# Relu² attention and a feed-forward block on one core: attention steps merged into two per head pair, first weights averaged a chunk ahead, tokens kept in load order

## The chip, the core and the metric

One core of a Trainium2 chip runs the whole program. The metric is device microseconds (us) of one execution, the median of several. Engines are named as the profile names them: PE is TensorE's matmuls, PEld its weight loads, DVE is VectorE, ACT is ScalarE, POOL is GpSimd, SP is SyncE. The fast executions of one kernel in one set of rounds agree within 1.5 per cent here, most of them within one; an execution more than 1.5% above the fastest of its kernel is called slow and is left out of the ratios.

## The reference

```python
# q, k, v: (8, 12, 448, 64) float32; g_ln: (768,); w_ch1: (768, 3072); w_ch2: (3072, 768)
scores = (1 / sqrt(64)) * q @ k.T                    # per batch and head
attn   = relu(scores) ** 2 / 448
x      = (attn @ v).transpose(0, 2, 1, 3).reshape(8, 448, 768)
xn     = (x - mean(x)) / sqrt(var(x) + 1e-6) * g_ln  # over the last axis
out    = x + relu(xn @ w_ch1) @ w_ch2
```

## The kernel before

Heads are worked in pairs: 6 pairs in each of 8 batches, 48 in all. A pair goes through these steps on PE: `att_T` transposes its q and k (16 small matmuls), `att_QK(i, t)` makes scores for one of four groups of 112 keys (two matmuls; four such steps a pair), and `att_AV` multiplies by the values (8 matmuls) and accumulates. ScalarE applies the relu to each score tile, VectorE squares it, and VectorE writes the pair's result into `xT`, the transposed input of the feed-forward block.

The mean of the layer norm is folded into the first weights: `prep_w1` averages a chunk of `w1` (6 matmuls) and rewrites it with six VectorE operations. There are six chunks, and each is averaged once, during the first projection of batch 0. `ffn_1` is one block of the first layer (6 matmuls with a 448-wide operand), `ffn_x` transposes `xT` back to tokens for the residual, `ffn_2` is a quarter of an output tile of the second layer.

PE's order is fixed by the program. Attention steps are put between the blocks of the feed-forward layers.

```python
NJ = 4; SP = S // NJ                      # 4, 112: token = 4 * p + j
def load_batch(b, groups):                # q, k, v in `groups` equal pieces
    ...
def prep_w1(c):
    mean_ps = ps_f.tile([P, CH], fp32, tag="f")
    for ki in range(K1):
        nc.tensor.matmul(mean_ps, gmat[:, ki, :], w1[:, ki, c * CH:(c + 1) * CH], ...)
    for ki in range(K1):
        nc.vector.scalar_tensor_tensor(w1[:, ki, c * CH:(c + 1) * CH], ..., g_sb[:, ki:ki + 1], mean_ps,
                                       op0=Alu.mult, op1=Alu.subtract)
def att_QK(i, t):
    at = attn_pool.tile([SP, 2, S], bf16, tag="attn")     # 8 buffers
    sc = ps_sc.tile([P, 2, 512], fp32, tag="sc")          # 2 buffers
    ...                                                   # two matmuls
    nc.scalar.activation(at, sc[:SP, :, :S], Act.Relu)
    nc.vector.tensor_mul(at, at, at)
def att_AV(i):
    ps = ps_m.tile([P, S], fp32, tag="m")                 # 2 buffers, shared with att_T and ffn_x
    ...                                                   # eight matmuls
    nc.vector.tensor_scalar(
        xT[b][:, pr, :].rearrange("c (p j) -> c j p", j=NJ),
        ps[:, :].rearrange("c (j p) -> c j p", j=NJ), c2, None, op0=Alu.mult)
...
for i in range(NP_ALL):                                   # four excursions a pair
    att.append(att_T(i + 1));  att.append(att_QK(i, 0), att_QK(i, 1))
    att.append(att_AV(i - 1)); att.append(att_QK(i, 2), att_QK(i, 3))    # shortened
...
if u == 0 and bb == 0 and ni % (K2 // NCH) == 0:          # directly before the chunk's own blocks
    ffn.append((u * U + bb, 0.0, lambda c=ni // (K2 // NCH): prep_w1(c)))
...
load_batch(0, 3); load_batch(1, 2)                        # shortened
for c in range(2):
    load_w1(c)
```

## Time and profile before

| | before |
|---|---|
| median time | 640.27 us (3 runs, 639.38 to 642.77) |
| span of the profiled run, and its own time | 643.6 us, 645.38 us |
| mean granted clock of the profiled run | 0.981 |
| PE busy | 95% of the span |

From the page of the kernel before: the busy line, and four groups. A group's columns are line, engine, operation, output and inputs, shapes and count; then total busy us and mean ns; then the engine's idle time just before these instructions and what ended most of it.

```profile
PE 609.9 (95%) x4255; PEld 307.6 (48%) x4260; DVE 289.1 (45%) x476; ACT 283.6 (44%) x418; POOL 36.8 (6%) x49
...
L206 PE MATMUL ps<-xT_t,w_112 128*128 128x448 bf16 x1152 | 248.5, 362 | 14.8 <-DVE w_112 L117 13.9
...
L166 DVE TENSOR_SCALAR xT_t<-ps 128x448 bf16<-128x448 f32 x48 | 55.3, 1151 | 26.0 <-PE ps L161 25.9
...
L117 DVE SCALAR_TENSOR_TENSOR w_112<-w_112,g_sb,mean_ps 128x512 bf16<-128x512 bf16 x36 | 24.2, 739 | 1.3 <-PE mean_ps L114 1.3
```

The first layer (L206) waited 13.9 us for the scaling of its weights (L117). The write into `xT` (L166) takes 1.15 us each. An average over the span hides where this happens, so here is the table of windows of the kernel before: start and end, length, then busy us and instructions of PE, PEld, DVE, ACT and POOL, then granted clock, DMA share and GB/s.

```profile
0.00:36.00 36.00, 23.08 (x233) 12.25 (x234) 26.40 (x49) 23.06 (x27) 19.24 (x30) 1.00 1.23 170
36.00:60.00 24.00, 18.68 (x93) 7.03 (x94) 13.79 (x21) 7.36 (x12) 3.50 (x5) 0.93 1.33 203
60.00:90.00 30.00, 23.04 (x105) 8.49 (x107) 16.82 (x27) 10.00 (x15) 0.00 (x0) 0.83 0.87 157
90.00:121.00 31.00, 26.74 (x187) 12.00 (x187) 19.42 (x33) 17.05 (x24) 2.04 (x3) 0.83 0.34 45
...
160.00:640.00 480.00, 479.51 (x3348) 249.25 (x3346) 193.65 (x317) 199.95 (x299) 9.41 (x11) 1.00 0.20 40
```

From 160 us on PE is practically never idle (479.5 of 480 us). From 36 to 121 us it is busy 68.5 of 85 us, and part of that is at a lowered clock. So a gain in the first 121 us has to come from waits, and a gain after that has to come from PE's own work.

In the second part PE's own work still holds something to remove. The timeline of PE in the kernel before, in its steady part (start, duration, what ran):

```profile
140.82 2.44 PE L206 MATMUL ps<-xT_t,w_112 128*128 128x448 bf16 x12
143.19 0.59 PE L147 MATMUL sc<-qkT_t 64*112 64x448 bf16 x4
143.71 2.44 PE L206 MATMUL ps<-xT_t,w_112 128*128 128x448 bf16 x12
146.08 0.39 PE L133 MATMUL ps<-identity,q_sb 112*64 112x112 bf16 x8
```

From start to start, twelve first-layer matmuls take 2.37 us (143.19 less 140.82) and four score matmuls 0.52. Where 36 first-layer matmuls stand in a row they take 6.81 us, 0.189 each, so twelve alone should take 2.27. What is over comes with a change of tile shape (128x128 here, 64x112 and 112x64 in attention). Over the whole steady part in program order the prediction counts 483.7 us of matmul and 283 changes in 518.5 us; what is over gives 0.123 us a change.

Attention of batch 0 is bound by VectorE. Its timeline in one head pair of the kernel before:

```profile
20.44 1.17 DVE L150 TENSOR_TENSOR at<-at 112x896 bf16<-112x896 bf16 x2
21.54 0.61 DVE L139 COPY qkT_t<-ps 128x896 bf16<-128x896 bf16 x1
22.07 1.15 DVE L150 TENSOR_TENSOR at<-at 112x896 bf16<-112x896 bf16 x2
23.15 1.17 DVE L166 TENSOR_SCALAR xT_t<-ps 128x448 bf16<-128x448 f32 x1
```

There is no idle time in it, and the pattern repeats after 3.67 us (24.11, not shown, less 20.44).

### The profile page before, as it was taken

What the parts mean: (1) busy time and instruction counts of PE and PEld (TensorE: products, weight loads), DVE (VectorE), ACT (ScalarE), POOL (GpSimd) and SP (SyncE); (2) the same over time, 40 slices, a digit from 0 to 9 for tenths busy, and PEclk for the clock granted to TensorE, in tenths of its full rate; (3) what the DMA queues carried; (4) which work ended last, traced back from release to release, by engine and by line L of the source; (5) the groups of instructions that cost most, each with busy time, mean ns of one, the idle gap of its engine ahead of it and who ended that gap; (6) DMA issues with size and microseconds to landing.
All of it is one profiled execution on the core that took longest, in us unless ns stands there. A gap on an engine that the chain in (4) does not pass through costs nothing.

```text
span 643.6 us, 9809 instructions
## 1 busy us (share of the span) xinstructions
PE 609.9 (95%) x4255; PEld 307.6 (48%) x4260; DVE 289.1 (45%) x476; ACT 283.6 (44%) x418; POOL 36.8 (6%) x49
## 2 busy tenths in 40 slices
PE   4777878899999999999999999999999999999997
PEld 2422333444555544444555554444555555555664
DVE  4966455754545444455544443554554310112111
ACT  3933334766332346767433326676634105552000
POOL 7330001001000100001000100000000000000000
PEclk9989787999999999999999999999999999999999
DMA  9999910900641173006220813000001110000111
GB/s 130 201 203 206 210 26 0 129 1 4 109 74 44 50 111 43 0 2 87 32 62 25 135 36 58 2 1 1 1 25 50 49 50 2 0 1 25 50 50 49
DMA packets 45483, 37.59 MB, mean 58 GB/s; under 512 B 1920, under 2 KB 41856, under 8 KB 45440
## 3 DMA queue, kind: packets, MB, share of 16 engines
q0 software_dynamic: 40624, 25.96, 28.5%
q1 hardware_dynamic: 4816, 11.01, 4.4%
q8 instruction: 33, 0.54, 0.4%
q14 instruction: 10, 0.08, 0.0%
HBM read 51.91 MB, written 11.01 MB: 98 GB/s over the span
## 4 chain that ended last, share of the span: by engine, by line
PE 88%; DVE 9%; ACT 1%; DMA 1%; issue 1%; POOL 0%; POOLq 0%; ACTq 0%
PE ps L206 35%; PE o_ps L222 35%; PE sc L147 6%; PE ps L161 6%; DVE w_112 L117 4%; PE ps L133 3%; DVE at L150 2%; PE ps L190 2%; DVE xT_t L166 1%; DMA k_sb<-in_k_dram 1%; ACT at L149 1%; DVE qkT_t L139 1%; PE mean_ps L114 1%; DVE stats L197 0%; POOL q_sb L91 0%
## 5 line engine op out<-in xcount | busy, mean ns | idle before, releaser
L206 PE MATMUL ps<-xT_t,w_112 128*128 128x448 bf16 x1152 | 248.5, 362 | 14.8 <-DVE w_112 L117 13.9
L222 PE MATMUL o_ps<-w_113,h_114 128*128 128x384 bf16 x1344 | 230.9, 327 | 0.0
L149 ACT ACTIVATE at<-sc 112x896 bf16<-112x896 f32 x192 | 164.5, 918 | 129.6 <-PE sc L147 129.5
L150 DVE TENSOR_TENSOR at<-at 112x896 bf16<-112x896 bf16 x192 | 118.8, 624 | 156.5 <-ACT at L149 156.5
L208 ACT ACTIVATE h_114<-ps 128x448 bf16<-128x448 f32 x192 | 105.0, 547 | 167.4 <-PE ps L206 167.4
L206 PEld LDWEIGHTS <-w_112 128*128 128x128 bf16 x1152 | 107.3, 99 | 136.3 <-DVE w_112 L117 26.4
L222 PEld LDWEIGHTS <-h_114 128*128 128x128 bf16 x1344 | 125.7, 98 | 97.9 <-issue 19.0
L225 DVE SCALAR_TENSOR_TENSOR o_t<-o_ps,rstd_t,x_t 128x384 f32<-128x384 f32 x56 | 34.5, 616 | 74.2 <-PE o_ps L222 74.0
L166 DVE TENSOR_SCALAR xT_t<-ps 128x448 bf16<-128x448 f32 x48 | 55.3, 1151 | 26.0 <-PE ps L161 25.9
L147 PE MATMUL sc<-qkT_t 64*112 64x448 bf16 x384 | 59.8, 381 | 5.9 <-ACT at L149 5.9
L161 PE MATMUL ps<-at,v_sb 112*64 112x448 bf16 x384 | 48.5, 369 | 1.2 <-DVE at L150 0.5
L196 DVE BATCH_NORM_STATS2 stats<-x_t 128x6 f32<-128x384 bf16 x28 | 15.7, 561 | 64.0 <-ACT x_t L193 63.7
L139 DVE COPY qkT_t<-ps 128x896 bf16<-128x896 bf16 x48 | 29.8, 620 | 23.8 <-PE ps L133 23.3
L147 PEld LDWEIGHTS <-qkT_t 64*112 64x112 bf16 x384 | 19.7, 127 | 38.2 <-issue 36.9
L161 PEld LDWEIGHTS <-v_sb 112*64 112x64 bf16 x384 | 19.0, 112 | 26.6 <-issue 19.8
L133 PE MATMUL ps<-identity,q_sb 112*64 112x112 bf16 x384 | 19.4, 226 | 6.2 <-DMA q_sb<-in_q_dram 6.2
L117 DVE SCALAR_TENSOR_TENSOR w_112<-w_112,g_sb,mean_ps 128x512 bf16<-128x512 bf16 x36 | 24.2, 739 | 1.3 <-PE mean_ps L114 1.3
L193 ACT COPY x_t<-ps 128x768 bf16<-128x768 bf16 x28 | 22.5, 803 | 3.3 <-PE ps L190 3.3
L133 PEld LDWEIGHTS <-q_sb 112*64 112x64 bf16 x384 | 12.1, 113 | 21.1 <-issue 14.6
L91 POOL DMA_DIRECT2D q_sb<-in_q_dram x11 | 9.4, 859 | 217.8 <-PE ps L133 216.6
L133 PE MATMUL ps<-identity,k_sb 112*64 112x112 bf16 x384 | 18.3, 220 | 1.4 <-DMA k_sb<-in_k_dram 1.4
L91 POOL DMA_DIRECT2D v_sb<-in_v_dram x11 | 9.3, 844 | 117.1 <-PE ps L161 116.3
(23 smaller groups left out, 95.8 us busy)
## 6 DMA issues: line engine op xcount, KB each, us to landing
out_dram<-o_t SPq DMA_DIRECT2D x28, 384.0 KB, 2.3
w_112<-in_moe_w_ch_dram POOLq DMA_DIRECT2D x6, 768.0 KB, 22.0
w_113<-in_moe_w_ch_dram POOLq DMA_DIRECT2D x4, 1152.0 KB, 33.9
q_sb<-in_q_dram POOLq DMA_DIRECT2D x6, 672.0 KB, 7.3
k_sb<-in_k_dram POOLq DMA_DIRECT2D x6, 672.0 KB, 10.3
v_sb<-in_v_dram POOLq DMA_DIRECT2D x6, 672.0 KB, 7.2
q_sb<-in_q_dram POOLq DMA_DIRECT2D x3, 224.0 KB, 7.5
k_sb<-in_k_dram POOLq DMA_DIRECT2D x3, 224.0 KB, 8.0
```

What stands on the lines that cost most here:

```text
L117: nc.vector.scalar_tensor_tensor(w1[:, ki, c * CH:(c + 1) * CH], w1[:, ki, c * CH:(c + 1) * CH], g_sb[:, ki:ki + 1], mean_ps, op0=Alu.mult ...
L133: nc.tensor.transpose(ps[hh * D:(hh + 1) * D, t, j * SP:(j + 1) * SP], sb[:, 2 * pr + hh, j * D:(j + 1) * D], identity[:SP, :SP])
L139: nc.vector.tensor_copy(qkT[i], ps)
L147: nc.tensor.matmul(sc[:SP, hh, :S], qkT[i][r, 1, t * SP:(t + 1) * SP], qkT[i][r, 0, :], start=True, stop=True)
L149: nc.scalar.activation(at, sc[:SP, :, :S], Act.Relu)
L150: nc.vector.tensor_mul(at, at, at)
L161: nc.tensor.matmul(ps[hh * D:(hh + 1) * D, :], v_sb[:, 2 * pr + hh, t * D:(t + 1) * D], attn[i, t][:, hh, :], start=(t == 0), stop=(t == N ...
L166: nc.vector.tensor_scalar(xT[b][:, pr, :].rearrange("c (p j) -> c j p", j=NJ), ps[:, :].rearrange("c (j p) -> c j p", j=NJ), c2, None, op0 ...
L206: nc.tensor.matmul(ps, w1[:, ki, ni * P:(ni + 1) * P], xT[u * U + bb][:, ki, :], start=(ki == 0), stop=(ki == K1 - 1))
L208: nc.scalar.activation(h1[:, ni, bb * S:(bb + 1) * S], ps, Act.Relu)
L222: nc.tensor.matmul(o_sb[1], h1[:, ki, m * P:(m + 1) * P], w2[:, ki, j * hd:(j + 1) * hd], start=(ki == 0), stop=(ki == K2 - 1))
L225: nc.vector.scalar_tensor_tensor(o_sb[0][:, j * hd:(j + 1) * hd], o_sb[1], rstd[u][:, m:m + 1], x_tok[u][:, m, j * hd:(j + 1) * hd], op0=A ...
```

## The change

It has six parts. The four excursions per pair become two, and a pair's values stand next to the transposes of a later pair, because both have 112x64 tiles. The attention steps are spread by deadlines instead of by a rate. Each chunk's average stands a chunk ahead of its use, the first one inside batch 0's attention, with its own accumulator pool. `xT` keeps the order in which tokens are loaded, so the write is contiguous and the output goes out in two or three pieces. Half of batch 1's squares go to GpSimd. Loads of batch 0 come in groups of 2, 4 and 6 heads. The diff, cut to its core:

```diff
-    def load_batch(b, groups):               # equal groups
+    def load_batch(b, groups):               # for hs in groups: ...
...
     def prep_w1(c):
-        mean_ps = ps_f.tile([P, CH], fp32, tag="f")
+        mean_ps = ps_m.tile([P, CH], fp32, tag="m")
...
         nc.scalar.activation(at, sc[:SP, :, :S], Act.Relu)
-        nc.vector.tensor_mul(at, at, at)
+        eng = nc.gpsimd if (NPAIR <= i < 2 * NPAIR and t % 2 == 1) else nc.vector
+        eng.tensor_mul(at, at, at)
...
         nc.vector.tensor_scalar(
-            xT[b][:, pr, :].rearrange("c (p j) -> c j p", j=NJ),
-            ps[:, :].rearrange("c (j p) -> c j p", j=NJ), c2, None, op0=Alu.mult)
+            xT[b][:, pr, :], ps, c2, None, op0=Alu.mult)
...
-                nc.sync.dma_start(out_flat[r0:r0 + P, :], o_sb[0])
+                while c0 < (m + 1) * P:      # one piece per group of 112 columns
+                    ...
+                    nc.sync.dma_start(out_tok[u * U + bb, ..., jj, :], o_sb[0][...])
...
-        att.append((b, lambda i=i: (att_QK(i, 0), att_QK(i, 1))))
-        ...                                  # four excursions a pair
+    def step_a(i):
+        att_QK(i, 0)
+        att_QK(i, 1)
+    def step_b(i):
+        att_QK(i, 2)
+        att_QK(i, 3)
+        if i > 0:
+            att_AV(i - 1)
+        if i + 2 < NP_ALL:
+            att_T(i + 2)
...
-                if u == 0 and bb == 0 and ni % (K2 // NCH) == 0:
-                    ffn.append((u * U + bb, 0.0, lambda c=ni // (K2 // NCH): prep_w1(c)))
+                if u == 0 and bb == 0 and ni % CPN == 0 and ni // CPN + 1 < NCH:
+                    items.append((0.0, lambda c=ni // CPN + 1: prep_w1(c)))
...
-    load_batch(0, 3)
-    load_batch(1, 2)
-    for c in range(2):
+    load_batch(0, (2, 4, 6))
+    load_batch(1, (6, 6))
+    for c in range(NCH):
         load_w1(c)
...
+        while ai < steps_of(0):
+            if ai == steps_of(0) - 4:
+                prep_w1(0)
+            pull()
...                                          # then pull() whenever ai + 1 <= target(t)
```

More of the change, by code (lines that the diff above doesn't have):

```diff
@@ L45 @@
     c2 = (1.0 / D) / S
-    out_flat = out.rearrange("b s d -> (b s) d")
+    out_tok = out.rearrange("b (p j) d -> b p j d", j=NJ)
     const_pool = ctx.enter_context(tc.tile_pool(name="const", bufs=1))
@@ L87, in load_batch @@
         v_sb = io_pool.tile([SP, H, NJ * D], bf16, tag="v_sb")
-        hs = H // groups
-        for gi in range(groups):
+        h0 = 0
+        for hs in groups:
             for sb, src in ((q_sb, q), (k_sb, k), (v_sb, v)):
                 nc.gpsimd.dma_start(
-                    sb[:, gi * hs:(gi + 1) * hs, :],
-                    src[b, gi * hs:(gi + 1) * hs].rearrange("h (p j) d -> p h (j d)", j=NJ),
+                    sb[:, h0:h0 + hs, :],
+                    src[b, h0:h0 + hs].rearrange("h (p j) d -> p h (j d)", j=NJ),
                 )
+            h0 += hs
         qkv[b] = (q_sb, k_sb, v_sb)
@@ L228, in ffn_2 @@
             if j == 1:
-                r0 = u * UT + m * P
-                nc.sync.dma_start(out_flat[r0:r0 + P, :], o_sb[0])
-    att = []
-    NP_ALL = B * NPAIR
-    att.append((0, lambda: att_T(0)))
-    for i in range(NP_ALL):
-        b = i // NPAIR
-        if i + 1 < NP_ALL:
-            att.append((b, lambda i=i: att_T(i + 1)))
-        att.append((b, lambda i=i: (att_QK(i, 0), att_QK(i, 1))))
-        if i > 0:
-            att.append(((i - 1) // NPAIR, lambda i=i: att_AV(i - 1)))
-        att.append((b, lambda i=i: (att_QK(i, 2), att_QK(i, 3))))
@@ L244 @@
-    att.append((B - 1, lambda: att_AV(NP_ALL - 1)))
+                c0 = m * P
+                while c0 < (m + 1) * P:
+                    g0 = c0 // SP
+                    c1 = min((m + 1) * P, (g0 + 1) * SP)
+                    bb, jj = divmod(g0, NJ)
+                    nc.sync.dma_start(
+                        out_tok[u * U + bb, c0 - g0 * SP:c1 - g0 * SP, jj, :],
+                        o_sb[0][c0 - m * P:c1 - m * P, :])
+                    c0 = c1
+    NP_ALL = B * NPAIR
+    att = []
@@ L246, with steps_of @@
+    def step_a(i):
[8 more added lines that the diff above has]
+            att_T(i + 2)
+    for i in range(NP_ALL):
+        att.append(lambda i=i: step_a(i))
+        att.append(lambda i=i: step_b(i))
+    att.append(lambda: att_AV(NP_ALL - 1))
+    def steps_of(b):
+        return min(len(att), 2 * NPAIR * (b + 1) + 2) if b < B - 1 else len(att)
     NU = B // U
-    ffn = []
+    segs = []
@@ L248 @@
+    CPN = K2 // NCH
     for u in range(NU):
-        last = u * U + U - 1
         for bb in range(U):
+            items = []
             for ni in range(K2):
-                if u == 0 and bb == 0 and ni % (K2 // NCH) == 0:
-                    ffn.append((u * U + bb, 0.0, lambda c=ni // (K2 // NCH): prep_w1(c)))
-                ffn.append((u * U + bb, 1.12, lambda u=u, bb=bb, ni=ni: ffn_1(u, bb, ni)))
+                if u == 0 and bb == 0 and ni % CPN == 0 and ni // CPN + 1 < NCH:
+                    items.append((0.0, lambda c=ni // CPN + 1: prep_w1(c)))
+                items.append((1.12, lambda u=u, bb=bb, ni=ni: ffn_1(u, bb, ni)))
@@ L255 @@
                 if ni % 6 == 5:
-                    m = bb * 4 + ni // 6
-                    m -= 1 if bb == 0 else 1
+                    m = bb * 4 + ni // 6 - 1
                     if 0 <= m < MU:
-                        ffn.append((u * U + bb, 0.4, lambda u=u, m=m: ffn_x(u, m)))
+                        items.append((0.4, lambda u=u, m=m: ffn_x(u, m)))
+            segs.append((u * U + bb, items))
+        items = []
         for m in range(MU):
@@ L262 @@
                 for part in range(4):
-                    ffn.append((last, 0.96, lambda u=u, m=m, j=j, p=part: ffn_2(u, m, j, p, 4)))
-    load_batch(0, 3)
-    load_batch(1, 2)
+                    items.append((0.96, lambda u=u, m=m, j=j, p=part: ffn_2(u, m, j, p, 4)))
+        segs.append((u * U + U - 1, items))
+    load_batch(0, (2, 4, 6))
+    load_batch(1, (6, 6))
+    for c in range(NCH):
+        load_w1(c)
+    ai = 0
     nload = 2
-    for c in range(2):
-        load_w1(c)
     def pull():
-        nonlocal nload, ai
-        b, fn = att[ai]
-        fn()
+        nonlocal ai, nload
+        att[ai]()
@@ L275, in pull @@
         ai += 1
-        if ai < len(att):
-            done = att_done(ai)
-            while nload < B and nload - 2 < done:
-                load_batch(nload, 1)
-                nload += 1
-    last_av = {}
-    for n, (b, _) in enumerate(att):
-        last_av[b] = n
-    def att_done(n):
-        c = 0
-        while c < B and last_av[c] < n:
-            c += 1
-        return c
-    ai = 0
-    with tc.manual_schedule(engines={mybir.EngineType.PE}):
-        total = sum(c for need, c, _ in ffn if need < B - 2)
-        nfree = 0
-        credit = 0.0
-        wc = 2
-        w2c = 0
-        for n, (need, cost, fn) in enumerate(ffn):
-            while att_done(ai) <= need:
-                pull()
-            if nfree == 0:
-                nfree = len(att) - ai
-                rate = nfree / (total * 1.0)
-            fn()
-            if cost == 0.0:
-                if wc < NCH:
-                    load_w1(wc)
-                    wc += 1
-                elif w2c == 0:
-                    while w2c < W2C:
-                        load_w2(w2c)
-                        w2c += 1
-            credit += cost * rate
-            while credit >= 1.0 and ai < len(att):
-                pull()
-                credit -= 1.0
-        assert ai == len(att) and nload == B and w2c == W2C
@@ new lines, in pull, with target @@
+        while nload < B and ai >= steps_of(nload - 2):
+            load_batch(nload, (6, 6))
+            nload += 1
+            if nload == 3:
+                for c in range(W2C):
+                    load_w2(c)
+    with tc.manual_schedule(engines={mybir.EngineType.PE}):
+        att_T(0)
+        att_T(1)
+        while ai < steps_of(0):
+            if ai == steps_of(0) - 4:
+                prep_w1(0)
+            pull()
+        bounds = {}
+        total = 0.0
+        cum = []
+        for need, items in segs:
+            total += sum(c for c, _ in items)
+            cum.append(total)
+        t1 = cum[0]
+        t_end = cum[-1] - sum(c for c, _ in segs[-1][1]) - sum(c for c, _ in segs[-2][1])
+        n0, n1, n2 = steps_of(0), steps_of(1), len(att)
+        def target(t):
+            if t <= t1:
+                return n0 + (n1 - n0) * t / (t1 - 3.0)
+            return n1 + (n2 - n1) * (t - t1) / (t_end - 3.0 - t1)
+        t = 0.0
+        for need, items in segs:
+            while ai < steps_of(need):
+                pull()
+            for cost, fn in items:
+                fn()
+                t += cost
+                while ai < len(att) and ai + 1 <= target(t):
+                    pull()
+        assert ai == len(att) and nload == B
```

## The prediction

> **What bounds it now.** The page gives TensorE (PE) 95% of the 643.6 us span and 88% of the chain. By stage (table of windows, chain in order of time):
>
> - 0 to 36 us: attention of batch 0, bound by VectorE. Per head pair: four squares (0.5 us each), one strided write into xT (1.10), one transpose copy (0.54); 3.68 us a pair.
> - 36 to 121: first projection of batch 0. Each of six weight chunks is averaged on PE, scaled by six VectorE operations (4.05 us in a row) and used at once. PE waits for them (13.9 us in 30 waits); granted clock falls to 0.50 to 0.85 in several 5 us stretches. It ends with a VectorE-bound burst (110 to 121) that catches up batch 1's attention.
> - 121 to 640: PE without a gap. 36 first-layer matmuls take 6.81 us, 12 take 2.38: 0.19 each plus 0.12 whenever the next block has another tile shape. Four score matmuls take 0.52 for 0.38. The Trainium skill, "TensorEngine Tiling (Array Packing)", Key Properties, says a change of tiling mode drains the TensorE; the 0.12 agrees. In program order I count 483.7 us of matmul and 283 changes; at 0.123 each that gives the measured 518.5.
>
> **What changes.**
> 1. Four excursions per pair (8 changes) become two: scores; scores, values, transposes. Values and transposes share the column-tiled shape, so I count 5 changes. After batch 0's projection 283 become about 184: 99 x 0.123 = 12 us, all on the critical path.
> 2. The average moves a chunk ahead, so its 4 us of VectorE runs under PE work. A chunk then costs 24 matmuls (4.54), an average (1.29), a pair's attention (1.91) and changes: 8.4 us; six take 50, where 36 to 121 went by, and no catch-up burst remains.
> 3. The write into xT becomes contiguous: 1.10 to about 0.55 us, an estimate from the 0.62 of the 384-wide output operation. Batch 0's attention becomes ScalarE-bound: four relus of 0.865, 3.5 us a pair.
> 4. Half of batch 1's squares go to GpSimd. The skill, "GPSIMD Engine Reference", section 4.1, calls it about 2x slower for two-input elementwise; I estimate 2 to 2.5 us each. Needed a pair later, so hidden.
> 5. Outputs leave in two or three pieces per tile; tail unchanged.
>
> **The new cost.** The first average now stands in PE's order before pair 5. By the DMA rates in the windows (200 GB/s), q, k, v of two batches land at 26.5 us and weight chunk 0 near 30.5; PE is there at about 27.5 and waits 3 to 4 us. The six scalings then delay pair 5's squares, and the first projection starts near 41 instead of 36.5.
>
> **Sum.** First layer starts at 41, then 557 us of matmul and changes by the same count, 2 of small waits (the average needs an accumulator that xT's write frees), 4 of tail: span 604; the timed runs lie 3 below the span: 601 us, 6% faster. About 27 us come from the start, 12 from fewer changes.
>
> **Signs.** PE's waits on weight scaling vanish; a 2 to 5 us wait on the weight DMA appears near 28; clock 1.0 after 45 us; batch 0's projection ends near 92; blocks of score, value and transpose take 1.9 us; the xT write 0.5 to 0.65.
>
> **What would break it.** Score to value changes dearer than 0.123; GpSimd squares queued behind weight DMA issues, stalling the values of pairs 6 to 8; the clock staying low; ScalarE holding first-layer evictions.

## More of the kernel before

The span is what the profiler sees of one execution. The time of that same execution is 1.8 us longer.

## The result, and the profile after

| | before | after |
|---|---|---|
| median time of the same rounds | 641.52 us (4 runs, 639.38 to 643.46) | 622.73 us (4 runs, 620.59 to 623.85) |
| span of the profiled run | 643.6 us | 622.1 us |
| its own time | 645.38 us | 623.85 us |
| its granted clock | 0.981 | 0.988 |

The ratio is 0.9704, with a 95% interval of 0.9658 to 0.9749: faster by 3.0%. A ratio here and below is the mean time of one kernel's fast runs over that of the kernel before in the same rounds, so it is not quite the ratio of the medians that are quoted. The prediction said 601 us. The direction was right, the gain is half of what was forecast, and the time is 21.7 us above the predicted one.

The same lines of the page of the kernel after:

```profile
PE 588.5 (95%) x4254; PEld 316.8 (51%) x4260; DVE 259.6 (42%) x464; ACT 284.9 (46%) x418; POOL 68.3 (11%) x79
...
L208 PE MATMUL ps<-xT_t,w_112 128*128 128x448 bf16 x1152 | 231.1, 354 | 1.0 <-DVE xT_t L169 0.7
...
L169 DVE TENSOR_SCALAR xT_t<-ps 128x448 bf16<-128x448 f32 x48 | 29.4, 613 | 4.8 <-PE ps L164 4.8
...
L119 DVE SCALAR_TENSOR_TENSOR w_112<-w_112,g_sb,mean_ps 128x512 bf16<-128x512 bf16 x36 | 24.3, 741 | 6.4 <-PE mean_ps L116 6.4
```

The first layer lost its waits (14.8 to 1.0 us of idle time before it) and 17.4 us of busy time; fewer changes of shape and less time at a lowered clock would both act on it, and the page doesn't part them. The `xT` write fell from 1.15 to 0.61 us. These three signs are as predicted. The windows of the kernel after:

```profile
0.00:36.00 36.00, 20.62 (x187) 11.15 (x189) 19.46 (x39) 18.02 (x21) 18.93 (x30) 1.00 1.21 168
36.00:60.00 24.00, 16.67 (x128) 8.21 (x128) 19.95 (x26) 11.99 (x16) 13.01 (x11) 0.82 1.29 205
60.00:90.00 30.00, 27.42 (x189) 13.12 (x192) 21.09 (x35) 16.14 (x24) 12.03 (x10) 0.92 1.22 198
90.00:121.00 31.00, 30.44 (x234) 15.61 (x233) 19.07 (x32) 21.21 (x33) 6.06 (x5) 1.00 0.22 29
...
160.00:617.00 457.00, 455.31 (x3241) 248.07 (x3239) 163.58 (x304) 196.03 (x292) 15.20 (x20) 1.00 0.20 38
```

From 90 us on PE is nearly without a gap, as forecast. The first row is worse than before: in the first 36 us PE ran 187 matmuls where the kernel before ran 233. In the second it runs more than before (128 to 93), but it is idle for 7.3 us and its granted clock is 0.82. PE's waits in the kernel after (total us, times, longest), the groups that matter:

```profile
PE sc L149 <- ACT at L151: 7.0, 14, 0.8
...
PE mean_ps L116 <- DVE xT_t L169: 6.0, 4, 4.7
...
PE ps L192 <- DVE xT_t L169: 2.5, 3, 0.8
```

One of the waits of an average for an `xT` write is 4.7 us long. It ends at 60.52, and the next three fences show PE, DVE and POOL of the kernel after around it. A bracket gives the idle time before the instruction and what ended it.

```profile
60.52 0.59 PE L116 MATMUL mean_ps<-w_112,gmat 128*128 128x512 bf16 x1 [4.71 <-DVE xT_t L169]
61.33 1.91 PE L116 MATMUL mean_ps<-w_112,gmat 128*128 128x512 bf16 x4 [0.22 <-issue]
63.03 3.36 PE L208 MATMUL ps<-xT_t,w_112 128*128 128x448 bf16 x12
```

```profile
55.45 4.48 DVE L153 TENSOR_TENSOR at<-at 112x896 bf16<-112x896 bf16 x1 [1.97 <-ACT at L151]
59.86 0.61 DVE L169 TENSOR_SCALAR xT_t<-ps 128x448 bf16<-128x448 f32 x1
```

```profile
55.28 0.82 POOL L111 DMA_DIRECT2D w_113<-in_moe_w_ch_dram  x1 [0.94 <-DMA k_sb<-in_k_dram]
56.12 3.33 POOL L153 TENSOR_TENSOR at<-at 112x896 bf16<-112x896 bf16 x2
```

A square that elsewhere takes VectorE 0.62 us took 4.48 us. It ended at 59.93, 0.48 us after both GpSimd squares had ended (56.12 plus 3.33). Four other VectorE squares (at 44.67, 87.48, 95.50 and 97.93) met one on GpSimd; they took 1.25 to 1.90 us, and each ended 0.48 us after it. The `xT` write stood behind it on VectorE, the average of the third chunk stood behind that write, because it takes the accumulator that the write frees, and PE sat idle. After the gap twelve first-layer matmuls took 3.36 us instead of 2.43: the clock had dropped.

The slower start is seen on ScalarE, whose relus were to be the limit. Its timeline in the kernel after, one line for each head pair:

```profile
16.86 3.35 ACT L151 ACTIVATE at<-sc 112x896 bf16<-112x896 f32 x4 [0.53 <-PE sc L149]
22.24 3.35 ACT L151 ACTIVATE at<-sc 112x896 bf16<-112x896 f32 x4 [2.02 <-PE sc L149]
27.57 3.34 ACT L151 ACTIVATE at<-sc 112x896 bf16<-112x896 f32 x4 [1.98 <-PE sc L149]
31.38 3.34 ACT L151 ACTIVATE at<-sc 112x896 bf16<-112x896 f32 x4 [0.47 <-PE sc L149]
```

Four relus take 3.35 us, as predicted, but the pairs follow each other after 5.38, 5.33 and 3.81 us, because ScalarE waits for the next pair's scores. PE shows why, in the second of those pairs:

```profile
18.64 0.62 PE L149 MATMUL sc<-qkT_t 64*112 64x448 bf16 x2 [0.19 <-ACT at L151]
19.19 1.71 PE L164 MATMUL ps<-at,v_sb 112*64 112x448 bf16 x8
21.57 0.99 PE L149 MATMUL sc<-qkT_t 64*112 64x448 bf16 x4
```

Between the last scores of a pair and the first of the next stand the values and the transposes (19.19 to 21.57, the transposes of 0.59 us twice are not shown). Two score buffers keep ScalarE busy for two relus, 1.7 us, and PE took 2.4 us. Values took 1.71 us there and 0.95 at the full clock; four scores 0.99 and 0.59.

The steady part of the kernel after looks as intended: values and transposes follow each other without a change of shape.

```profile
166.22 0.58 PE L149 MATMUL sc<-qkT_t 64*112 64x448 bf16 x4
166.73 0.95 PE L164 MATMUL ps<-at,v_sb 112*64 112x448 bf16 x8
167.51 0.36 PE L135 MATMUL ps<-identity,q_sb 112*64 112x112 bf16 x8
```

Counted in program order, the whole program has 348 changes of shape before and 230 after.

### The profile page after: what moved, and what is told of

It reads as the page before. It is cut to its first block, busy times and chain, and to the rows that moved or that the text cites. A ratio compares the mean times of both kernels' runs of the same rounds, so it can differ in the third digit from the quotient of the medians.

```text
span 622.1 us, 9876 instructions
## 1 busy us (share of the span) xinstructions
PE 588.5 (95%) x4254; PEld 316.8 (51%) x4260; DVE 259.6 (42%) x464; ACT 284.9 (46%) x418; POOL 68.3 (11%) x79
## 4 chain that ended last, share of the span: by engine, by line
PE 88%; DVE 4%; ACT 3%; issue 2%; DMA 1%; POOL 1%; POOLq 0%; ACTq 0%
PE o_ps L224 36%; PE ps L208 35%; PE sc L149 7%; PE ps L164 5%; ACT at L151 3%; PE ps L135 3%; PE mean_ps L116 2%; DVE at L153 1%; PE ps L192 1%; DVE w_112 L119 1%; DMA k_sb<-in_k_dram 1%; DVE xT_t L169 1%; ACT x_t L195 0%; ACT h_114 L210 0%; POOL q_sb L92 0%
## 5 line engine op out<-in xcount | busy, mean ns | idle before, releaser
L208 PE MATMUL ps<-xT_t,w_112 128*128 128x448 bf16 x1152 | 231.1, 354 | 1.0 <-DVE xT_t L169 0.7
L224 PE MATMUL o_ps<-w_113,h_114 128*128 128x384 bf16 x1344 | 225.0, 326 | 0.0
L224 PEld LDWEIGHTS <-h_114 128*128 128x128 bf16 x1344 | 128.5, 98 | 89.4 <-issue 6.1
L208 PEld LDWEIGHTS <-w_112 128*128 128x128 bf16 x1152 | 108.7, 98 | 106.9 <-issue 11.8
L149 PE MATMUL sc<-qkT_t 64*112 64x448 bf16 x384 | 61.3, 390 | 7.0 <-ACT at L151 7.0
L164 PE MATMUL ps<-at,v_sb 112*64 112x448 bf16 x384 | 47.8, 372 | 0.4 <-DVE w_112 L119 0.4
L169 DVE TENSOR_SCALAR xT_t<-ps 128x448 bf16<-128x448 f32 x48 | 29.4, 613 | 4.8 <-PE ps L164 4.8
L92 POOL DMA_DIRECT2D q_sb<-in_q_dram x17 | 13.1, 769 | 149.7 <-PE ps L135 147.6
L92 POOL DMA_DIRECT2D v_sb<-in_v_dram x17 | 12.9, 761 | 134.4 <-PE ps L164 133.4
L135 PEld LDWEIGHTS <-q_sb 112*64 112x64 bf16 x384 | 16.5, 117 | 15.3 <-DMA q_sb<-in_q_dram 6.6
L153 POOL TENSOR_TENSOR at<-at 112x896 bf16<-112x896 bf16 x12 | 20.9, 1744 | 24.8 <-ACT at L151 24.8
```

The source lines that it names most:

```text
L135: nc.tensor.transpose(ps[hh * D:(hh + 1) * D, t, j * SP:(j + 1) * SP], sb[:, 2 * pr + hh, j * D:(j + 1) * D], identity[:SP, :SP])
L149: nc.tensor.matmul(sc[:SP, hh, :S], qkT[i][r, 1, t * SP:(t + 1) * SP], qkT[i][r, 0, :], start=True, stop=True)
L153: eng.tensor_mul(at, at, at)
L164: nc.tensor.matmul(ps[hh * D:(hh + 1) * D, :], v_sb[:, 2 * pr + hh, t * D:(t + 1) * D], attn[i, t][:, hh, :], start=(t == 0), stop=(t == N ...
L169: nc.vector.tensor_scalar(xT[b][:, pr, :], ps, c2, None, op0=Alu.mult)
L208: nc.tensor.matmul(ps, w1[:, ki, ni * P:(ni + 1) * P], xT[u * U + bb][:, ki, :], start=(ki == 0), stop=(ki == K1 - 1))
```

## The experiments

My theory after the trace: most of the missing 22 us lies before 63 us, and it comes in four pieces. The GpSimd squares hold VectorE; the merged order starves ScalarE in the start, made worse by a cold clock; the load groups 2, 4, 6 start the pairs late; and waits for `xT` writes come back wherever an average or a token transpose follows a merged block. Rivals: a change of shape is worth less than 0.123 us, so that merging gains little anywhere; the clock alone makes the start slow; the arrival of the first weight chunk alone paces it. All twelve kernels gave the reference's result. The runs came in three sets of four, each set on one chip with the kernel before; the medians of the kernel before were 641.42 (e1 to e4), 640.73 (e5 to e8) and 642.78 us (e9 to e12). Kernels of different sets, and after with any of them, are best compared by their ratios; differences of medians are given as such and can be off by a microsecond or two.

| run | edit | median us | ratio to before (95%) |
|---|---|---|---|
| e1_dve | after, no squares on GpSimd | 615.88 | 0.9609 (0.9571 to 0.9646) |
| e2_groups444 | after, loads of batch 0 in 4, 4, 4 | 622.32 | 0.9695 (0.9666 to 0.9724) |
| e3_split0 | after, pairs 1 to 6 in the old order | 616.15 | 0.9626 (0.9562 to 0.9690) |
| e4_four | after, four excursions everywhere | 625.16 | 0.9736 (0.9711 to 0.9762) |
| e5_defer | e1, average or token transposes not directly after a merged block | 614.78 | 0.9574 (0.9533 to 0.9614) |
| e6_warm | e1, filler matmuls in the start | 615.36 | 0.9587 (0.9542 to 0.9631) |
| e7_early | e1 + e2 + e3, first chunk loaded and averaged early | 616.22 | 0.9608 (0.9570 to 0.9645) |
| e8_best | e7 + e5 | 612.69 | 0.9557 (0.9518 to 0.9596) |
| e9_late | after, each chunk averaged directly before its use | 644.66 (one of four slow) | 1.0009 (0.9944 to 1.0074) |
| e10_strided | after, old `xT` write and output order | 624.93 | 0.9726 (0.9696 to 0.9756) |
| e11_split | e8, first chunk's scaling spread over the steps | 606.31 | 0.9435 (0.9406 to 0.9464) |
| e12_splitwarm | e11 + filler in the first 20 us | 608.59 | 0.9471 (0.9442 to 0.9500) |

### e1_dve: no squares on GpSimd

```diff
-        eng = nc.gpsimd if (NPAIR <= i < 2 * NPAIR and t % 2 == 1) else nc.vector
-        eng.tensor_mul(at, at, at)
+        nc.vector.tensor_mul(at, at, at)
```

> The changed kernel with all squares on VectorE. Theory: the GpSimd squares hold up VectorE's own squares (one took 4.48 us at 55.5 us, another 1.78), which delays the write into xT, which makes the third weight average wait 4.7 us, after which the clock is cold for some 4 us: expect every VectorE square at 0.5 to 0.7 us, no PE wait over 1.5 us after 50 us, and 6 to 10 us less than the changed kernel (613 to 617). Rival: VectorE was the scarce engine there, so 12 squares of 0.63 us more (7.5 us) come back as waits for weight scaling: no gain, or slower.

Measured: 615.88 us, 6.9 us less than after by the medians and 6.1 by the ratios (0.0095 of 641). PE in e1 at the place of the 4.7 us wait:

```profile
54.04 1.46 PE L116 MATMUL mean_ps<-w,gmat 128*128 128x512 bf16 x5 [0.85 <-DVE xT_t L168]
55.33 2.43 PE L207 MATMUL ps<-xT_t,w 128*128 128x448 bf16 x12
```

The wait is 0.85 us and the matmuls behind it run at full clock. All 192 squares now lie between 573 and 627 ns on VectorE; in the kernel after VectorE's 180 ranged up to 4483 ns. So the GpSimd squares cost about 6 us, through VectorE, and they were not needed: VectorE had the time. Of the two traces, e1 is 5.6 us shorter from the average of the second chunk to the end of PE (44.50 to 608.74, against 47.04 to 616.85). The first layer also began at 46.08 instead of 48.70 us, but that is not the edit's doing: the first average, which stands before any square on GpSimd, was already at 32.64 instead of 35.16, and from there to the first layer both kernels took 13.4 to 13.5 us. The shorter hold at 44.67 (1.78 us) cost next to nothing.

### e2_groups444: equal load groups

```diff
-    load_batch(0, (2, 4, 6))
+    load_batch(0, (4, 4, 4))
```

> The changed kernel with batch 0 loaded in groups of 4, 4, 4 heads in place of 2, 4, 6. Theory: the second pair's transposes stand before the first scores in PE's order, and with 2 heads first they need the second group too, so the first scores start at 12.3 us instead of 9.6: expect first scores near 9.6 and 2.5 to 3 us less (about 620). Rival: the start is paced by something later (weights, clock), and the 2.7 us vanish in a later wait: same time.

Measured: 622.32 us over five runs, the same as after. This expectation failed. The first scores came sooner and the attention of batch 0 ran 2.9 us ahead, but none of it reached the end: the first chunk's average then waited 1.45 us for its weights, and the second chunk's average waited 2.88 us for an `xT` write behind two VectorE squares that took 4.96 us beside GpSimd's. In this kernel an earlier start of the pairs only meets later waits. The load groups alone did not cost the kernel after any time that can be measured.

### e3_split0: the old order of steps, in pairs 1 to 6 only

```diff
     def step_a(i):
+        if 0 < i <= NPAIR:
+            att_T(i + 1)
...
     def step_b(i):
+        if 0 < i <= NPAIR:
+            att_AV(i - 1)
         att_QK(i, 2)
         att_QK(i, 3)
-        if i > 0:
+        if i > NPAIR:
             att_AV(i - 1)
-        if i + 2 < NP_ALL:
+        if NPAIR <= i and i + 2 < NP_ALL:
             att_T(i + 2)
```

> The changed kernel with the old interleaved order (transposes, scores, values, scores) for pairs 1 to 6 alone. Theory: in the attention-only phase the merged order puts 1.3 us (2.5 at the cold clock) of values and transposes between the last scores of a pair and the first of the next, more than the two score buffers cover, so ScalarE runs dry 0.5 to 2 us per pair: with the old order expect ScalarE gaps of 0.3 us, 3.7 us per pair instead of 4.0 to 5.4, first layer starting near 41 to 43 instead of 48.7, and 5 to 7 us less (616 to 618). Rival: the cold clock alone stretches the pairs, whatever the order: periods of 4.5 to 5.4 us remain and the time stays within 2 us of 622.

Measured: 616.15 us, 6.6 us less than after by the medians and 5.0 by the ratios (one of its four runs took 624.26, so its interval is wide). ScalarE in the start of e3:

```profile
18.25 12.06 ACT L151 ACTIVATE at<-sc 112x896 bf16<-112x896 f32 x14 [0.63 <-PE sc L149]
```

Fourteen relus in 12.06 us without a gap, 3.45 us a pair. That is the 3.5 us a pair that the prediction had claimed for the merged order. The estimate of ScalarE's work was right; the order of PE's steps did not allow it. What then stands in the way is the weights: the first average waits 2.6 us for its DMA, the wait that was predicted and is absent in the kernel after, and the values behind it wait 2.8 us for the scalings.

But the expectation about the start failed. The first layer was to begin at 41 to 43 us and began at 46.24, no sooner than in e1 (46.08), which has the merged order. The time came out as expected by luck: between the two profiled runs 8.5 us of span differ (622.1 and 613.6), and 6.0 of them lie behind the start of the first layer (48.70 to 616.85 in the kernel after, 46.24 to 608.40 in e3). The squares on GpSimd are still there in e3, but they met VectorE's at other moments: no VectorE square took more than 1.90 us, and the third average waited 0.85 us where the kernel after waited 4.71. The other runs of the two kernels have no trace, so whether they had the hold is not known.

```profile
54.20 1.46 PE L116 MATMUL mean_ps<-w,gmat 128*128 128x512 bf16 x5 [0.85 <-DVE xT_t L169]
```

So e3 shows that the order makes ScalarE's gaps. That the order costs the kernel after time is not shown by it.

### e4_four: four excursions everywhere

```diff
     for i in range(NP_ALL):
-        att.append(lambda i=i: step_a(i))
-        att.append(lambda i=i: step_b(i))
+        att.append(lambda i=i: att_T(i + 1) if 0 < i < NP_ALL - 1 else None)
+        att.append(lambda i=i: (att_QK(i, 0), att_QK(i, 1)))
+        att.append(lambda i=i: att_AV(i - 1) if i > 0 else None)
+        att.append(lambda i=i: (att_QK(i, 2), att_QK(i, 3)))
...                                          # and the step counts that go with it
```

> The changed kernel with four excursions per pair everywhere, still spread by deadlines and with weights a chunk ahead. Theory: each change of tile shape costs 0.12 us of PE time, three more per pair over 41 pairs is 15 us, and the start gains 5 us as in the run before: about 632. Rival: the merge is worth little (the drains hide behind weight loads): 616 to 619.

Measured: 625.16 us. I had expected about 632, so undoing the merge cost far less than that: e4 to after is 2.4 us by the medians, 2.1 by the ratios. The reason is only in small part a cheaper change of shape. From the first block of the first layer to the end of PE e4 takes 571.8 us (46.27 to 618.03) and e3, which is merged in this stretch, 562.2. Program order gives 332 changes there in e4 and 214 in e3. PE is busy for 569.3 and 556.4 us of it: 12.9 us for 118 changes, 0.11 each where 0.123 was counted. Against that, PE's named waits in this stretch are 2.4 us in e4 and 5.5 in e3, so merging brings 3.1 us of waits with it. That leaves 9.6 us of gain for e3. The kernel after has the same order as e3 here and takes 568.1 us: the long hold, which neither e3 nor e4 has (their longest VectorE squares took 1.90 and 1.58 us), takes 6.0 of them back. And its first layer began 2.4 us later than e4's, of which e1 shows that a like amount comes and goes without an edit.

### e5_defer: nothing that needs an accumulator directly behind a merged block

```diff
+            fresh, held = False, []
             for cost, fn in items:
-                fn()
                 t += cost
+                if fresh and cost < 0.9:          # average or token transposes
+                    held.append(fn)
+                    continue
+                fn()
+                fresh = False
+                for h in held:
+                    h()
+                held = []
                 while ai < len(att) and ai + 1 <= target(t):
+                    fresh = ai % 2 == 1           # the step just put in was a merged block
                     pull()
...                                          # what is still held at the end of a segment follows
```

> The run with all squares on VectorE, and in addition a weight average or a token transpose that would follow a scores-values-transposes block directly is emitted six first-layer matmuls later. Theory: such a block leaves both buffers of the shared accumulator pool in use, and what follows at once waits 0.85 us for the write into xT (seven waits of 0.33 to 0.85 us in that run, 4.5 us together): expect one or two of them left and 3 to 4.5 us less than that run (611.5 to 613). Rival: the wait only moves to the weights, whose scaling starts 1.1 us later and now has little slack: PE waits on weight scaling appear and the gain is under 1 us.

Measured: 614.78 us; against e1 the ratio falls from 0.9609 to 0.9574, 2.2 us. I had expected 611.5 to 613. The waits went as meant: token transposes for the `xT` write from 2.5 us to 0.8, averages from 1.7 to 0.9 (PE's waits from 47 us on), 2.5 us together. The remaining expected gain did not come; in the profiled run the first layer began at 47.49 us, 1.4 later than in e1. The first average stood at 34.74 already, against 32.64 in e1, and up to there the two programs are the same, so that part is not the edit's. The intervals of e1 and e5 overlap.

### e6_warm: is it the clock?

Filler matmuls that write an unused accumulator: ten after the first transposes and two between the score steps of pairs 0 to 6, on top of e1.

```diff
+    def warm(n):
+        ps = ps_f.tile([P, CH], fp32, tag="f")
+        for _ in range(n):
+            nc.tensor.matmul(ps..., gmat[:, 0, :], gmat[:, 0:4, :], start=True, stop=True)
...
     def step_a(i):
         att_QK(i, 0)
         att_QK(i, 1)
+        if i <= NPAIR:
+            warm(2)
```

> The run with all squares on VectorE, with idle PE time of the start filled by matmuls whose result nobody reads (ten of 512 columns after the first transposes, two between the score steps of pairs 0 to 6). Theory: the long pair periods (5.4 us against 3.8) are the cold clock, which the low PE activity of this order keeps cold: expect values blocks at 0.9 to 1.0 us instead of 1.7 from pair 1 on, pairs of 3.8 us, first-layer start 2 to 4 us earlier than 46.1, and 2 to 4 us less in all (612 to 614). Rival: order and ScalarE set the pace whatever the clock, and the filler delays real work: same time or slower.

Measured: 615.36 us, the same as e1. Two lines of PE in e6, a pair apart, and the first average:

```profile
18.91 0.59 PE L149 MATMUL sc<-qkT_t 64*112 64x448 bf16 x4
...
22.73 0.58 PE L149 MATMUL sc<-qkT_t 64*112 64x448 bf16 x4
...
31.97 2.31 PE L116 MATMUL mean_ps<-w,gmat 128*128 128x512 bf16 x5 [1.55 <-DMA w<-in_moe_w_ch_dram]
```

The pairs follow after 3.82 us instead of the 5.38 of the same pair in the kernel after (4.03 in e1), with the order unchanged. So the cold clock is what stretched the pairs: the order leaves 0.5 us a pair idle at the full clock, and 2.0 at the cold one. Yet the first layer began at 46.02 us, against 46.08 in e1. The first chunk landed at about 32 us, and its average and its scaling, which run as one block, set the start. The clock was a cause of slow pairs and not of the lost time.

### e7_early and e8_best: first chunk early, then all mends together

```diff
+    load_w1(0)                       # before batch 1 instead of after it
     load_batch(1, (6, 6))
-    for c in range(NCH):
+    for c in range(1, NCH):
         load_w1(c)
...
-            if ai == steps_of(0) - 4:
+            if ai == 4:
                 prep_w1(0)
```

> All squares on VectorE, old interleaved order for pairs 1 to 6, batch 0 in groups of 4, 4, 4 heads, and weight chunk 0 loaded before batch 1 and averaged after pair 1. Theory: with the order, groups and squares repaired, the first layer's start is paced by the arrival of weight chunk 0 (PE waited 1.45 and 2.63 us for it in the two runs that start early) and by its 4 us of scaling, which then stands in front of pair 5's squares: expect no PE wait for weights, first-layer start at 36 to 39 us instead of 46, and 7 to 9 us less than the runs at 616 (607 to 609). Rival: VectorE (six pairs of 3.1 us and 4 us) or batch 1's later arrival fill the gap: start at 43 or later, 614 or more.

Measured: 616.22 us. This missed clearly: the first layer was to begin at 36 to 39 us and began at 47.8. PE in e7:

```profile
20.41 2.72 PE L116 MATMUL mean_ps<-w,gmat 128*128 128x512 bf16 x6 [4.23 <-DMA w<-in_moe_w_ch_dram]
...
27.26 1.71 PE L163 MATMUL ps<-at,v_sb 112*64 112x448 bf16 x8 [2.97 <-DVE w L119]
```

At step 4 the average stood in PE's order 4.2 us before its weights were there. Then the six scalings, one block on VectorE, held back the squares that the values needed, for 3.0 us, and the clock was down behind the gaps (values 1.71 us). PE's order is fixed, so an average that is too early stops everything behind it.

e8 puts the deferral of e5 on top of e7 (no other edit).

> The run before together with the later emission of averages and token transposes. Theory: the gains are in different stretches and add: 603 to 606. Rival: the shorter slack between average and use of a chunk costs what the buffer waits gave: 607 to 609 as without it.

Measured: 612.69 us, 3.5 us less than e7 by the medians. The 603 to 606 that were expected took e7's gain for granted and were missed with it. With the two changes of e7 that went wrong it is still the best of the first eight.

### e9_late and e10_strided: two parts of the change undone

e9 puts each chunk's average back to where the kernel before had it; all else is as after.

```diff
-                if u == 0 and bb == 0 and ni % CPN == 0 and ni // CPN + 1 < NCH:
-                    items.append((0.0, lambda c=ni // CPN + 1: prep_w1(c)))
+                if u == 0 and bb == 0 and ni % CPN == 0:
+                    items.append((0.0, lambda c=ni // CPN: prep_w1(c)))
...
-            if ai == steps_of(0) - 4:
-                prep_w1(0)
```

> The changed kernel with one part undone: each weight chunk is again averaged and scaled directly before its own first use (the average still in the shared pool). Theory: the preparation a chunk ahead is the largest part of the gain: without it each of six chunks costs PE a 4 us serial scaling of which at most 1 us is hidden, and a cold clock after it, less some 4 us that the first scaling no longer takes out of batch 0's attention: expect PE waits on weight scaling of 12 us or more to return and 15 to 25 us more than the changed kernel (638 to 648). Rival: scaling was already hidden behind attention and the gain came from the layout and the order: under 630.

Measured: ratio 1.0009. Three fast runs took 639.99, 641.83 and 647.49 us; the profiled one took 650.43 and was slow, so its trace gives no times here. Against after the ratio rises by 0.0305, 20 us. Without the preparation a chunk ahead, all the rest of the change together gains nothing that can be measured.

e10 restores the strided write and the old token order.

```diff
-            xT[b][:, pr, :], ps, c2, None, op0=Alu.mult)
+            xT[b][:, pr, :].rearrange("c (p j) -> c j p", j=NJ),
+            ps[:, :].rearrange("c (j p) -> c j p", j=NJ), c2, None, op0=Alu.mult)
```

> The changed kernel with the other part undone: strided write into xT and outputs in the original token order. Theory: the write takes 1.15 us instead of 0.61; that lengthens each wait for it (four to seven of 0.85 us) by 0.5 us and batch 0's attention by at most 1 us in all, because ScalarE and the order pace it: 2 to 5 us more (625 to 628). Rival: VectorE paces the start and pays 0.5 us for every one of the first 12 pairs: 6 us or more.

Measured: 624.93 us, 2.2 us more than after by the medians, 1.4 by the ratios. The write saves 0.54 us in each of 48 pairs, 26 us of VectorE, and about 2 us of it showed in the time. The comparison is not clean, though: in e10's trace the long hold is at another place (two VectorE squares together 3.42 us from 43.77, and a second average that waits 2.33 us) and the square of 4.48 us is gone, so the write's own share isn't known.

### e11_split and e12_splitwarm: the scaling in pieces

e7 had shown that the first average must not come before its weights and that six scalings in a row hold up the squares. e11 is e8 with the average at step 7, in the first layer's accumulator pool, which is still unused, and one scaling after each of the next six attention steps. The new functions `prep_mean` and `prep_scale` are `prep_w1` cut in two.

```diff
-            if ai == 4:
-                prep_w1(0)
+            if ai == 7:
+                mean0 = prep_mean(0, ps_f, "f")
             pull()
+            if 8 <= ai < 8 + K1:
+                prep_scale(0, ai - 8, mean0)
```

> The run with all repairs at 612.7 us, with weight chunk 0 averaged one pair later (after its arrival at 20.4 us) into an idle first-layer accumulator, and its six scalings spread over six attention steps instead of in one block. Theory: the 4.0 us wait for the weights and the 2.3 us wait behind the block of scalings were what kept the first layer at 47.8 us: expect both gone, first layer at 39 to 42 and 606 to 609. Rival: the clock stays cold from 20 to 40 us and the pairs take 4.6 us as before: 45 or later, 611 or more.

Measured: 606.31 us (605.98 to 606.33), ratio 0.9435, granted clock 0.998. PE in e11:

```profile
21.96 1.47 PE L116 MATMUL mean_ps<-w,gmat 128*128 128x512 bf16 x5
...
38.04 1.46 PE L116 MATMUL mean_ps<-w,gmat 128*128 128x512 bf16 x5 [1.68 <-DVE xT_t L175]
39.33 2.43 PE L214 MATMUL ps<-xT_t,w 128*128 128x448 bf16 x12
```

The five matmuls at 21.96 had no gap before them, and the first layer begins at 39.33, 9.4 us sooner than after. This kernel beats the one before by 5.7% and the one after by 2.8% (0.9435 over 0.9704). Both expectations held. Of the 8.5 us between the profiled spans of e8 and e11 (613.1 and 604.6) all lie before the first layer, 47.84 against 39.33; from there to the end of PE both take 560.0 us. The place, the pool and the pieces were changed at once and are not told apart.

e12 adds filler matmuls to e11 in the first 20 us (four before the first transposes, two after them, two in each of the first three pairs).

```diff
+        warm(4)
         att_T(0)
+        warm(2)
         att_T(1)
```

> The run before with filler matmuls in the first 20 us (six of 512 columns around the first transposes, two per pair in pairs 0 to 2). Theory: clock warm from 12 us on, pairs of 3.5 us instead of 4.6: first layer 2 to 4 us earlier than without the filler and as much off the time (603 to 606). Rival: with the waits gone the clock warms by itself and the filler changes under 1 us.

Measured: 608.59 us, 2.3 us slower than e11, where 603 to 606 had been expected. The filler waited 4.0 us for its operand `gmat` and so put off what stood behind it: the first scores came at 10.61 us instead of 8.65. PE in e12 where e11 had 38.04:

```profile
38.98 2.16 PE L116 MATMUL mean_ps<-w,gmat 128*128 128x512 bf16 x5 [1.68 <-DVE xT_t L175]
```

The gap before it is the same 1.68 us, but here the matmuls ran slowly behind it.

## Why the prediction was right or wrong

The predicted sum was: first layer from 41 us, 557 us of matmul and changes, 2 of small waits, 4 of tail, less 3. I counted the 557 from the average of the second chunk, which opens that stretch. In the kernel after that average begins at 47.04 us, PE ends at 616.87, the span ends at 622.1, and the median is 622.73. The miss of 21.7 us splits on these marks:

| term of the sum | predicted us | measured us | off by |
|---|---|---|---|
| start of the stretch | 41 | 47.04 | 6.0 |
| stretch with its waits | 557 + 2 | 569.8 | 10.8 |
| tail | 4 | 5.2 | 1.2 |
| median less span | -3 | 0.6 | 3.6 |

**"The first projection starts near 41."** Wrong by 6.0 us; two steps failed. One is "Batch 0's attention becomes ScalarE-bound: ... 3.5 us a pair". It looked at the work of each engine and not at PE's new order. In the merged order PE's values and transposes keep ScalarE waiting between pairs, 0.5 us at the full clock and 2.0 at the cold one, and the pairs took 3.8 to 5.4 us. e3 shows it by the old order (3.45 us a pair), e6 by the clock (3.82). The first scores also came at 12.32 us instead of 9.56, because pair 1's transposes stand before them and wait for the second load group. So PE came to the first average at 35.16 us, not near 30.5. About 2.5 us of this come and go without an edit: e1, the same program up to there, came to it at 32.64.

The other is "The six scalings then delay pair 5's squares". From the first average to that of the second chunk the sum left 10.5 us (30.5 to 41); it took 11.9 in the kernel after and 13.4 in e3, where the old order had the first average start at 31.55. So neither the mended order (e3, 46.24) nor the warm clock (e6, 46.02) brought the first layer sooner than e1 (46.08), which has neither. e11, with the chunk loaded early, averaged once it is there and scaled in pieces, began it at 39.33. The predicted wait of 2 to 5 us on the weight DMA near 28 us did not appear in the kernel after, since PE came late; it is there in e3 (2.6 us) and e4 (3.3), where PE comes sooner.

**"Half of batch 1's squares go to GpSimd ... Needed a pair later, so hidden."** This is the step that failed worst. I cited section 4.1 of "GPSIMD Engine Reference" for the speed and overlooked what the same skill says of the ports: the Trainium skill, "SBUF — State Buffer", section "SBUF: two separate sides", calls the port pair of VectorE and GpSimd an exclusive lock against VectorE operations with two SBUF inputs, where the other "fully blocks". The trace agrees: 4.48 us instead of 0.62, ended 0.48 us after the GpSimd squares. The squares themselves took 1.68 us, even less than the estimated 2 to 2.5. Of the 10.8 us about 6 come from this one hold: 3.9 of wait (4.71 less the 0.85 that is left in e1), 1.2 in the average behind it (60.52 to 63.03, where e1 took 54.04 to 55.33), and 0.9 in the first twelve matmuls (3.36 less 2.43). e1, which removes the cause, gains 6.1 us by the ratios. The second item under "What would break it" had named GpSimd squares queued behind weight DMA issues, and the squares at 56.12 do stand behind such an issue. But the harm went through VectorE, not through late values.

**"2 of small waits."** Mis-sized. PE's waits from 62 us to the end sum to 4.7 us. Most of it is the accumulator that the prediction had named, 0.8 us each time an average or token transposes follow a merged block. e5 removed 2.5 us of such waits and gained 2.2 us over e1 by the ratios. Some 2 us of the 10.8 remain that I can't assign to a wait; matmul ends in a trace are modelled.

**"The timed runs lie 3 below the span."** An error of reading. It came from setting the median of before (640.27) against the span of one slower execution (643.6). That execution itself took 645.38: the time is 1.8 us longer than its own span. In the result the median lies 0.6 above the span.

**Changes of shape, 0.123 us each and "12 us, all on the critical path".** The cost was nearly right (0.11 by the busy time of e3 and e4). "Requires drain" in the Trainium skill's "TensorEngine Tiling (Array Packing)", Key Properties, agrees with it. That all of it is gain was wrong: merging brought back 3.1 us of waits in the long stretch, and the hold, which e4 escapes, took 6 more of what the merge had saved.

**The average a chunk ahead.** Right, and it carries the result: PE's 13.9 us of waits for the scaling are gone, and e9, which undoes it, loses 20 us. The prediction gave the start 27. Batch 0's projection ended at 106.4 us, not near 92. In the kernel before it ended at 110.0, and the burst of attention behind it lasted to 120.5.

**Clock "1.0 after 45 us".** Wrong until the hold was over: 0.82 from 36 to 60 us and 0.92 to 90. By the records it is 1.00 in every stretch of e11, though values took 1.71 us at 13.64 there too.

**Not settled.** Why the VectorE square at 55.45, whose record starts 0.66 us before the first GpSimd square, had to wait for both (a DMA issue on GpSimd alone is not the reason: in e1 39 VectorE squares run beside such issues and none takes more than 0.63 us); why identical beginnings differ by up to 2.5 us at the first average (after and e1: 1.0 us is there at the first scores, 12.32 and 11.32, and the rest comes with a clock that rose a pair later, values of 1.71 us at 24.56 and of 0.95 at 23.34); why the same 1.68 us gap was followed by slow matmuls in e12 and not in e11; how much of e11's earlier start is the order of its work and how much the clock, since both changed at once; and what the spreading of the attention steps by deadlines is worth, which every run kept.

## What to carry to other kernels

Work moved to an idle engine is free only if it shares nothing with the engine that it relieves: look for single instructions that grew far beyond their median, as the 4.48 us square did, before believing a busy-time budget. In a program with a fixed order on the main engine, merging steps saves its changes of shape but lengthens the stretch in which the next engine gets nothing, so merge where that engine has slack and keep the fine order where it is the limit (here that took the pairs from 3.8 to 5.4 us down to 3.45; what it alone is worth in time was not shown). A run that comes out as expected can do so for another reason, as e3 did: compare the traces stretch by stretch before crediting the edit. An operation placed early should be placed after its data arrives, and a block of helper work is best cut into pieces that fit between the steps: the two together were worth 6.4 us here by the medians, 7.8 by the ratios (e8 to e11).

## What the Trainium skill lacked or had wrong

- "TensorEngine Tiling (Array Packing)", Key Properties, says that a change of tiling mode drains TensorE and gives no cost. Here it is 0.11 to 0.12 us a change (e3 and e4, 118 changes and 12.9 us of busy time apart; 0.123 by the count of the kernel before). Values followed by transposes, both on 112x64 tiles, show none: eight values take 0.78 us there (166.73 to 167.51) and 0.88 before another shape (161.88 to 162.76 in the kernel before).
- "GPSIMD Engine Reference", section 4.1, says about 2x slower for two-input elementwise work. A 112x896 bf16 square took 1.68 us on GpSimd and 0.62 on VectorE, 2.7x. Section 4.1 doesn't repeat that the two engines also block each other.
- "SBUF — State Buffer", section "SBUF: two separate sides", has the lock right: all five VectorE squares that met one on GpSimd and were lengthened ended 0.48 to 0.49 us after it. It doesn't say who goes next when GpSimd runs two instructions in a row: at 55.45 us VectorE got its turn after both (4.48 us), and at 44.67 between them (it ended at 46.45, the first GpSimd square at 45.97, the second at 47.99).
- "TensorE: Matmul & The Clock Gate", section "Why this matters for your kernels", sets about 3 us of idle time as the limit. Here matmuls ran slowly after gaps of 1.55 us (e6: five in 2.31 us) and 1.68 us (e12: 2.16), and at full speed after 1.68 (e11: 1.46). The page gives no length for such shorter gaps. Its caveat that clock records can be unreliable agrees: the windows give 1.00 for the first 36 us of the kernel after, where values took 1.71 us instead of 0.95.
